# Ranking eight early steps by hand and loading the first units' queries without their zeros, in a kernel of chunked attention and a two-layer network

## The chip, the cores and the metric

The kernel runs on one core of one Trainium2 chip. A core has five engines, each with its own in-order queue: TensorE (PE, matmuls and their weight loads, the latter shown as PEld), VectorE (DVE), ScalarE (ACT), GpSimd (POOL) and SyncE (SP, which here only issues DMAs). They meet through semaphores. The metric is device time in microseconds (us), lower is better; the time before is the median of three runs.

## The reference

Attention over 4 batches, 8 heads, 768 positions, head size 64, in chunks of 32 queries; each chunk sees 8 memory keys, 16 positions to its left, itself and 8 to its right (at most 64 keys). The result, as 3072 tokens of 512 features, goes through a two-layer network of width 2048 with a leaky bend.

```python
for c in range(nc):
    l_start, r_end = max(0, c * 32 - 16), min(S, c * 32 + 40)
    k_full = concat([mem_k, k[:, :, l_start:r_end]]); v_full = concat([mem_v, v[:, :, l_start:r_end]])
    scores = matmul(q_c, k_full.T) / 8
    a = exp(scores - max(scores)); a = a / (sum(a) + 1e-09)
    out[:, :, c * 32:c * 32 + 32] = matmul(a, v_full)
x = out.transpose(0, 2, 1, 3).reshape(B * S, H * D)
h = x @ w_in
g = maximum(h, 0) + alpha * minimum(h, 0)
return g @ w_out
```

## The kernel before

**Units.** Attention is cut into 32 units: a pair of heads (4 pairs) by a block of 384 tokens (8 blocks, BT = 384). Four units fill x for one block. Units 0 to 7 (blocks 0 and 1) come first and go a way of their own, `windows` (L485 and on); the others are done in the shadow of the later matmuls.

**What a first unit goes through** (function `windows`): scores on PE (L307, 24 matmuls, ahead of them "stirs", L293, dummy matmuls on a tile of ones whose number is in STIR: eight for unit 0, two for others); `top`, a row maximum, on DVE (L504); `less`, the subtraction, on DVE (L508); `exps` on ACT (L512); `total` and `inverse` on DVE (L516, L519); `scale` on POOL in two steps (L529, L533); `turn`, one stir and six transposes on PE (L541); `keep`, two copies on ACT (L546); `values`, 16 matmuls on PE (L554); then x is split on ACT into a high part (L469) and on DVE into the low rest (L472). Units share buffers: score banks, exponentials, transposed weights and the tiles that `keep` fills are used in turn by even and odd units, and the loaded tile `early` by every fourth.

**A first unit's loads** (`load_first`, L485): one DMA of 1312 columns by 128 rows, the queries spread over two heads with zeros between them (768 columns, NQ) and the keys (544); another of 512 columns with the values. Keys and queries stand in DRAM as the kernel wants them, zeros included (array `first`, made in `_layout`). The score matmul takes 64 columns of the queries as its weights, contiguous in `early`: 32 queries of one head, 32 of the other, whose rows hold zeros where the other head's queries are.

**The weights** of the network come as 64-bit numbers, two DMAs for each of 16 slices f (w_in and w_out, L594), and are decoded on ACT and DVE: `rebias` (L617), `gather` (L625), `ends` (L629), `join` (L633), `high` (L641), `low` (L644). For f = 0 and 1 the two halves are decoded apart.

**The network.** Each place in ORDER is one (block, f): `up` (first layer, L718), `below` on ACT (L727), `bend` on DVE (L730), `high` and `low` (L736, L740), `down` (second layer, L748). Places 0 and 1 are f = 0 for blocks 0 and 1, places 2 and 3 are f = 1, and so on.

**Who sets the order.** Nothing runs in the order of the text. Every piece is a step of class `Plan`: engine, a cost, reads, writes, a due time. `Plan.send` gives each step a rank, the longest sum of costs and lags behind it, at least its due time; a user behind a DMA counts 2.3 us for the landing, one on another engine 0.07. Then it plays the plan: the engine that is free first takes, among its steps that are ready, the one of highest rank, the lower number where ranks are equal. What comes out is each engine's queue, which the chip runs in order. The steps are numbered in the order in which they are added: loads of units 0 to 3 and of the weights first, then unit by unit.

Of the kernel before, what the change touches and what calls it, by code (L numbers as in the profile page):

```python
# [18 lines left out]
P = 128  # L19
B, H, S, D = 4, 8, 768, 64  # L20
NM = 8
CH, LEFT, RIGHT = 32, 16, 8
# [3 lines left out]
NJ = TQ // CH  # L26
TK = LEFT + TQ + RIGHT
BT = 384
NHALF = B * S // BT
NT = BT // TQ  # L30
NPAIR = H // 2
# [36 lines left out]
NKT = TK + 2 * NM  # L68
STARTS = (0, LEFT + CH // 2, TK - 2 * CH + 2 * NM)

PE, DVE, ACT, POOL, SP = "PE", "DVE", "ACT", "POOL", "SP"
# [28 lines left out]
FIRST_FRONT = 12  # L100


STIR = (8, 2, 1)

DUE_WEIGHTS, LAST_OUT = 4, 8


NWIN, NSET = 2 * NPAIR, 4

STARTS_WIN = (0, 2 * LEFT, NKT - KW)  # L110
NQ = NT * NJ * 2 * CH
NV = NT * 2 * D
# [2 lines left out]


GATHER_ACT, HIGH_ACT = range(2, 14), 24


class Plan:  # L120
# [19 lines left out]
    def send(self):  # L140
        users = [[] for _ in self.steps]
        for n, step in enumerate(self.steps):
            for d in step[3]:
                users[d].append(n)
        lag = {PE: HOP, DVE: HOP, ACT: HOP, POOL: HOP, SP: LAND}
        behind = [0.0] * len(self.steps)
        for n in reversed(range(len(self.steps))):
            engine, cost, _, _, rest = self.steps[n]
            behind[n] = max(rest, cost + max((behind[m] + lag[engine] for m in users[n]), default=0.0))
        left = [len(step[3]) for step in self.steps]  # L150
        ready = [0.0] * len(self.steps)
        free = dict.fromkeys(lag, 0.0)
        able = {n for n in range(len(self.steps)) if not left[n]}
        while able:
            at = {}
            for n in able:
                engine = self.steps[n][0]
                at[engine] = min(at.get(engine, 1e9), max(ready[n], free[engine]))
            engine = min(at, key=at.get)
            n = max((n for n in able if self.steps[n][0] == engine and ready[n] <= at[engine]),  # L160
                    key=lambda n: (behind[n], -n))
            able.remove(n)
            _, cost, fn, _, _ = self.steps[n]
            free[engine] = at[engine] + cost
            fn()
            for m in users[n]:
                wait = lag[engine]
                if self.steps[m][0] == engine:
                    wait = FOLLOW if engine == DVE else 0.0
                ready[m] = max(ready[m], free[engine] + wait)  # L170
                left[m] -= 1
                if not left[m]:
                    able.add(m)
# [3 lines left out]
def body(ctx: ExitStack, tc: tile.TileContext, qvw, kw, first, w_in, w_out, alpha, out):  # L177
    nc = tc.nc
# [22 lines left out]
    qk = [const.tile([P, BT + NT * NKT], F32, name=f"qk{i}") for i in range(NKB)]  # L201
# [5 lines left out]
    early = [wps[NF - NSET + i, 0].tile([P, NQ + NT * NKT + NV], F32, name="early", tag="w") for i in range(NSET)]  # L207
# [7 lines left out]
        nc.gpsimd.memset(e[:, :, KW:], 1e-9)  # L215
    for ew in ews:
        nc.gpsimd.memset(ew, 0.0)
    warm = sm.tile([P, 1], F32, name="warm")
    nc.vector.memset(warm, 0.0)
    nc.scalar.activation(out=warm, in_=warm, func=AF.Exp)  # L220
# [2 lines left out]
    step = plan.add  # L223
# [20 lines left out]
    def rest(place):  # L244
        wide = NNARROW * NF
        return (len(ORDER) - max(place, wide)) * WIDE_PAIR + max(wide - place, 0) * PAIR

    def begins(u):

        return u // NPAIR if u < NWIN else BEGIN[(u - NWIN) // 2]  # L250

    def due(u, later=0):

        return rest(begins(u) + later + (5.5 if u >= FIRST_FRONT else 0))
# [35 lines left out]
    def stir(t, num):  # L290

        for _ in range(num):
            nc.tensor.matmul(out=t, lhsT=busy[:, :P], rhs=busy, start=True, stop=True)  # L293

    def score_products(u):
        blk, pr = divmod(u, NPAIR)
        st = state[u]
        s_ps = ps_s.tile([P, 512], F32, name="s_ps", tag=f"s{u % 2}")
        stir(s_ps, STIR[0] if u == 0 else STIR[1])
        st["s"] = s_ps[:, :2 * NJ * KW].rearrange("p (n k) -> p n k", k=KW)  # L300
        t = early[u % NSET]
        q = t[:, :NQ].rearrange("p (c x) -> p c x", c=NT * NJ)
        keys = t[:, NQ:NQ + NT * NKT].rearrange("p (t k) -> p t k", t=NT)
        for n in range(2 * NJ):
            for i in range(2):
                t, j = n // NJ * 2 + i, n % NJ
                nc.tensor.matmul(  # L307
                    out=st["s"][i * 2 * CH:(i + 1) * 2 * CH, n],
                    lhsT=q[:, t * NJ + j],
                    rhs=keys[:, t, STARTS_WIN[j]:STARTS_WIN[j] + KW],  # L310
                    start=True, stop=True,
                )
# [167 lines left out]
    def load_first(u):  # L480
        blk, pr = divmod(u, NPAIR)
        t = early[u % NSET]

        def load(lo, hi):
            nc.sync.dma_start(out=t[:, lo:hi], in_=first[blk, pr, :, lo:hi])  # L485

        state[u] = {}
        step(SP, 1.6, partial(load, 0, NQ + NT * NKT), writes=[("qk", u % NSET)], rest=due(u))
        step(SP, 0.78, partial(load, NQ + NT * NKT, NQ + NT * NKT + NV), writes=[("fv", u % NSET)], rest=due(u))

    def windows(u):

        st = state[u]
        sk, tks, ak = ("s", u % 2), [("o", 0), ("o", 1)], ("o", 2) if u % 2 else "a"
# [41 lines left out]
        def turn():  # L536
            st["t"] = [ps_o.tile([P, DM], F32, name="o_ps", tag=f"o{i}") for i in range(2)]
            stir(st["t"][0], STIR[2])
            for t in range(2):
# [8 lines left out]
        def values():  # L548
# [3 lines left out]
            for t in range(NT):  # L552
                for h2 in range(2):
# [4 lines left out]
                        start=True, stop=True,  # L558
                    )

        step(PE, 1.2, partial(score_products, u), reads=[("qk", u % NSET)], writes=[sk], rest=due(u))
        step(DVE, 0.66, top, writes=[sk, ("mx", u % 3)])
        step(DVE, 0.55, less, reads=[sk, ("mx", u % 3)], writes=e_keys(u))
        step(ACT, 0.52, exps, writes=e_keys(u))
# [24 lines left out]
    def load_w(f):  # L589
        def load(i):  # L590
            k, j = ((f, i), 0) if f < NAPART else ((f, 0), i)
            if k not in raw:
                raw[k] = wps[k].tile([P, 2 if f >= NAPART else 1, DM, 2], I32, name="w_t", tag="w")
            nc.sync.dma_start(out=raw[k][:, j].rearrange("p m b -> p (m b)"), in_=srcs[i][f])  # L594

        i = f - NF + NSET
        after = [("qk", i), ("fv", i)] if i >= 0 else []
        for i in range(2):
            step(SP, 1.31, partial(load, i), writes=[("r", f, i)] + after, rest=rest(place_of(f)))

    def place_of(f):
        return PLACE[0, f]
# [302 lines left out]
def _layout(q, k, v, mem_k, mem_v, moe_w_in, moe_w_out, moe_alpha):  # L905
    import numpy as np

    nh = S // BT
    qT = q.reshape(B, NPAIR, 2, nh, BT, D).transpose(0, 3, 1, 2, 5, 4)
    pad = ((0, 0), (0, 0), (LEFT, RIGHT), (0, 0))  # L910
    kp, vp = np.pad(k, pad), np.pad(v, pad)

    def keys(x, mem, s, *spans):
        return np.concatenate([mem if p is None else x[:, :, s + LEFT + p[0]:s + LEFT + p[1]] for p in spans], axis=2)

    kwin = np.stack([keys(kp, mem_k, t * TQ, (-16, 16), None, (16, 72), None, (72, 104)) for t in range(S // TQ)],
                    axis=2)
    kwin = kwin.reshape(B, NPAIR, 2, nh, NT, NKT, D).transpose(0, 3, 1, 2, 6, 4, 5)
    vwin = np.stack([keys(vp, mem_v, t * TQ, (-16, 16), None, (16, 104)) for t in range(S // TQ)], axis=2)
    vwin = vwin.reshape(B, NPAIR, 2, nh, NT, P, D).transpose(0, 3, 1, 5, 4, 2, 6)  # L920
    nwin = NWIN // NPAIR
    qd = np.zeros((nwin, NPAIR, 2, D, NT * NJ, 2, CH), q.dtype)
    for h in range(2):
        qd[:, :, h, :, :, h] = qT.reshape(NHALF, NPAIR, 2, D, NT * NJ, CH)[:nwin, :, h]
    kfirst = np.stack([keys(kp, mem_k, t * TQ, (-16, 16), None, (16, 104), None) for t in range(S // TQ)], axis=2)
    kfirst = kfirst.reshape(B, NPAIR, 2, nh, NT, NKT, D).transpose(0, 3, 1, 2, 6, 4, 5)
    kfirst = kfirst.reshape(NHALF, NPAIR, P, NT * NKT)[:nwin]
    vparts = vwin.reshape(NHALF, NPAIR, P, NV)
    return dict(
        qvw=np.concatenate([qT.reshape(NHALF, NPAIR, P, BT), vparts], axis=3),  # L930
        kw=np.ascontiguousarray(kwin).reshape(NHALF, NPAIR, P, NT, NKT),
        first=np.concatenate([qd.reshape(nwin, NPAIR, P, NQ), kfirst, vparts[:nwin]], axis=3),
        w_in=np.ascontiguousarray(moe_w_in.reshape(NK, P, NF, P).transpose(2, 1, 0, 3)
                                  ).reshape(NF, P, NK * P).view(np.int64),
        w_out=np.ascontiguousarray(moe_w_out.reshape(NF, P, DM)).view(np.int64),
        alpha=np.ascontiguousarray(moe_alpha.reshape(NF, P).T),
    )
# [15 lines left out]
```

## Time and profile before

| | us |
|---|---|
| median of 3 runs (599.72 to 600.05) | 600.02 |
| the profiled execution, whole | 600.83 |
| its span, first to last instruction | 599.0 |
| PE busy in the span | 592.1 |
| DVE, ACT, POOL busy | 388.2, 211.1, 36.7 |
| HBM read, MB | 41.95 |

The profile is of one execution, and its time of 600.83 us lies around a span of 599.0 us. A row of the order of time reads: start, length, engine, line of the kernel, operation, out<-in, shape, number of instructions, and in brackets the idle time of the engine just before and what ended it. A row of the DMA issues gives the kilobytes of each and the median time from issue to landing. A row by stretches gives for each engine the busy time within a window. The granted TensorE clock was 1.00 in the whole span.

### The profile page before, as it was taken

Reading aid. Unit: us, or ns where it says so; the run is one execution under the profiler, and the core shown is the slowest. Engines: PE = TensorE matmul, PEld = TensorE weight load, DVE = VectorE, ACT = ScalarE, POOL = GpSimd, SP = SyncE. Lnnn points to the kernel's source line nnn. Section 1 sums busy time; section 2 is a strip of 40 time slices with the busy share of each in tenths; the row PEclk is TensorE's granted clock in tenths of the full one; section 3 lists DMA queues with packets and bytes.
Section 4 is the critical chain, followed back from the end, with each engine's and each line's share of the span. In section 5 each row is a group of like instructions: output and inputs, shape, how many; then the busy total and the mean of one; then the engine's idle time right before and its main releaser. Section 6 shows DMA issues by size and latency. Waiting matters only on the chain.

```text
span 599.0 us, 10981 instructions
## 1 busy us (share of the span) xinstructions
PE 592.1 (99%) x4430; PEld 506.3 (85%) x4430; DVE 388.2 (65%) x904; ACT 211.1 (35%) x580; POOL 36.7 (6%) x61
## 2 busy tenths in 40 slices
PE   8999999999999999999999999999999999999997
PEld 5689898988988989899898888888888888888886
DVE  5888998887958768785885852861762771530530
ACT  3688878644222414323233301302400411210201
POOL 3410000010001101010010100100100100000000
PEclk9999999999999999999999999999999999999999
DMA  8999500222040302403204003003201000000001
GB/s 325 354 402 407 236 0 1 66 65 89 2 146 8 100 5 98 143 11 100 84 17 143 11 1 92 9 0 101 69 2 36 0 1 36 36 1 0 1 1 71
DMA packets 21076, 48.96 MB, mean 82 GB/s; under 512 B 2464, under 2 KB 5792, under 8 KB 21024
## 3 DMA queue, kind: packets, MB, share of 16 engines
q1 hardware_dynamic: 20880, 48.12, 22.7%
q8 instruction: 35, 0.57, 0.4%
q10 hardware_dynamic: 144, 0.13, 0.1%
q14 instruction: 17, 0.14, 0.1%
HBM read 41.95 MB, written 6.29 MB: 81 GB/s over the span
## 4 chain that ended last, share of the span: by engine, by line
PE 96%; DMA 2%; DVE 1%; ACT 1%; issue 0%; SPq 0%; ACTq 0%
PE h_ps L718 44%; PE o_ps L748 44%; PE a_ps L433 3%; PE s_ps L332 2%; DMA w_t<-w_in 2%; PE s_ps L293 1%; PE s_ps L307 1%; PE a_ps L554 0%; DVE w_t L629 0%; ACT qk L546 0%; PE o_ps L541 0%; ACT a L617 0%; DVE w_t L625 0%; DVE xl L472 0%; SPq L485 0%
## 5 line engine op out<-in xcount | busy, mean ns | idle before, releaser
L718 PE MATMUL h_ps<-xh,w 128*128 128x384 f32 (+1 forms) x896 | 248.8, 359 | 0.3 <-DVE w L644 0.3
L718 PEld LDWEIGHTS h_ps<-xh,w 128*128 128x128 f32 x896 | 164.8, 188 | 16.6 <-DVE w L644 0.6
L748 PE MATMUL o_ps<-w,gh 128*128 128x512 f32 x528 | 162.7, 389 | 0.0
L718 PE MATMUL h_ps<-xl,w 128*128 128x384 f32 (+1 forms) x448 | 162.6, 363 | 0.1
L727 ACT ACTIVATE g<-h_ps 128x384 f32<-128x384 f32 (+1 forms) x112 | 60.7, 542 | 194.4 <-PE h_ps L718 128.6
L730 DVE SCALAR_TENSOR_TENSOR g<-g,rise,h_ps 128x384 f32<-128x384 f32 (+1 forms) x112 | 74.8, 668 | 74.5 <-ACT g L727 73.6
L748 PEld LDWEIGHTS o_ps<-w,gh 128*128 128x128 f32 x528 | 99.1, 188 | 20.4
L408 DVE STREAM_TRANSPOSE pt<-e 32x64 f32<-32x64 f32 (+1 forms) x336 | 99.4, 301 | 7.4 <-POOL e L387 2.0
L748 PE MATMUL o_ps<-w,gl 128*128 128x512 f32 x264 | 102.8, 389 | 0.0
L718 PEld LDWEIGHTS h_ps<-xl,w 128*128 128x128 f32 x448 | 84.1, 188 | 10.2 <-DVE xl L472 0.3
L748 PE MATMUL o_ps<-w,xh 128*128 128x512 f32 x240 | 74.8, 393 | 0.0
L748 PEld LDWEIGHTS o_ps<-w,gl 128*128 128x128 f32 x264 | 49.6, 188 | 10.2
L472 DVE TENSOR_TENSOR xl<-a_ps,xh 128x384 fp32r<-128x384 f32 x32 | 17.7, 557 | 59.5 <-ACT xh L469 58.8
L748 PEld LDWEIGHTS o_ps<-w,xh 128*128 128x128 f32 x240 | 45.0, 188 | 8.9
L469 ACT CAST xh<-a_ps 128x384 fp32r<-128x384 f32 x32 | 15.0, 481 | 95.7 <-PE a_ps L433 93.7
L736 DVE CAST gh<-g 128x512 fp32r<-128x512 f32 (+1 forms) x72 | 28.8, 401 | 30.6 <-PE o_ps L748 28.2
L387 POOL TENSOR_TENSOR e<-e,den 128x384 f32<-128x384 f32 x24 | 22.7, 947 | 419.8 <-DVE den L384 270.0
L740 DVE TENSOR_TENSOR gl<-g,gh 128x512 fp32r<-128x512 f32 (+1 forms) x72 | 46.6, 648 | 1.7
L366 ACT ACTIVATE e<-s_ps,mx 128x64 f32<-128x64 f32 x144 | 43.4, 318 | 11.1 <-DVE mx L358 11.1
L748 PE MATMUL o_ps<-w,xl 128*128 128x512 f32 x120 | 46.8, 390 | 0.0
L366 ACT ACTIVATION_READ_ACCUMULATOR e<-s_ps,mx 128x1 f32 x144 | 30.4, 211 | 0.0
L805 ACT COPY o_t<-o_ps 128x512 f32<-128x512 f32 x21 | 12.2, 591 | 44.6 <-PE o_ps L748 44.1
(58 smaller groups left out, 382.6 us busy)
## 6 DMA issues: line engine op xcount, KB each, us to landing
w_t<-w_in SPq DMA_DIRECT2D x16, 512.0 KB, 10.1
w_t<-w_out SPq DMA_DIRECT2D x16, 512.0 KB, 10.0
qk<-kw SPq DMA_DIRECT2D x24, 272.0 KB, 4.4
v_t<-qvw SPq DMA_DIRECT2D x24, 256.0 KB, 2.9
out<-o_t SPq DMA_DIRECT2D x23, 256.0 KB, 2.1
early<-first SPq DMA_DIRECT2D x8, 656.0 KB, 6.3
qk<-qvw SPq DMA_DIRECT2D x24, 192.0 KB, 4.9
early<-first SPq DMA_DIRECT2D x8, 256.0 KB, 6.9
```

What stands on the lines that cost most here:

```text
L366: nc.scalar.activation(out=st["e"][:, i], in_=st["s"][h2][:, n], func=AF.Exp, scale=SCALE, bias=d["mx"][:, u - us[0], n, h2:h2 + 1], accum ...
L387: nc.gpsimd.tensor_tensor(out=st["e"], in0=st["e"], in1=st["den"].broadcast_to([P, NJ * 2, KW]), op=ALU.mult)
L408: nc.vector.transpose(out=pts[u % NPT][quad * CH:(quad + 1) * CH, j, t0:t0 + n1 - n0].rearrange("p t h q -> p (t h) q"), in_=(st["e"], zer ...
L433: nc.tensor.matmul(out=st["a"][h2 * D:(h2 + 1) * D, t * TQ:(t + 1) * TQ], lhsT=st["v"][:, t, h2, :], rhs=pts[u % NPT][:, :, t, h2, :], sta ...
L469: nc.scalar.copy(out=ring[k][0][:, cols], in_=st["a"][:, :BT])
L472: nc.vector.tensor_tensor(out=ring[k][1][:, cols], in0=st["a"][:, :BT], in1=ring[k][0][:, cols].bitcast(F32), op=ALU.subtract)
L718: nc.tensor.matmul(out=h["ps"][:, :n_cols], lhsT=ws[f, 0][:, wk, k * P:(k + 1) * P], rhs=parts(blk, k)[1](xk), start=(k == 0 and n == 0), ...
L727: nc.scalar.activation(out=h["g"], in_=h["ps"][:, :n_cols], func=AF.Relu, scale=-1.0)
L730: nc.vector.scalar_tensor_tensor(out=h["g"], in0=h["g"], scalar=rise[:, f:f + 1], in1=h["ps"][:, :n_cols], op0=ALU.mult, op1=ALU.add)
L736: copy(out=h["gh"], in_=h["g"])
L740: nc.vector.tensor_tensor(out=h["gl"], in0=h["g"], in1=h["gh"].bitcast(F32), op=ALU.subtract)
L748: nc.tensor.matmul(out=o_ps[tt], lhsT=h[gk][:, tt * P:(tt + 1) * P], rhs=ws[f, 1][:, wk], start=(f == first_f and i == 0), stop=(f == last ...
```

## The change

The queries of units 0 to 7 are stored in DRAM without zeros and loaded in two halves, one head's 64 rows each, into a tile whose other quarters are set to zero once by eight memsets on DVE. Inside the tile the queries of one column group now stand 12 columns apart, where they stood side by side. `load_first` adds four steps in place of two, with planned costs of 0.43 (three times) and 0.65 in place of 1.6 and 0.78; the score step waits for all three of its loads, and so does the weight load that later takes over the tile's place. The stirs ahead of unit 0's scores are seven. And after the ranks are worked out, eight steps get a number added to their own rank, by their step number: SHIFT.

```diff
-STIR = (8, 2, 1)
+STIR = (7, 2, 1)
...
+SHIFT = {11: -2.4, 14: -0.5, 53: -1.4, 92: -8.1, 137: -4.4, 188: 6.2, 195: 7.0, 231: -13.4}
...
             behind[n] = max(rest, cost + max((behind[m] + lag[engine] for m in users[n]), default=0.0))
+        for n, more in SHIFT.items():
+            behind[n] += more
...
+    for t in early:
+        for h2 in range(2):
+            nc.vector.memset(t[(1 - h2) * D:(2 - h2) * D, h2 * BT:(h2 + 1) * BT], 0.0)
...
-        q = t[:, :NQ].rearrange("p (c x) -> p c x", c=NT * NJ)
+        q = t[:, :NQ].rearrange("p (x c) -> p c x", c=NT * NJ)
...
-        def load(lo, hi):
-            nc.sync.dma_start(out=t[:, lo:hi], in_=first[blk, pr, :, lo:hi])
+        def load(rows, to, lo, hi):
+            nc.sync.dma_start(out=t[rows, to:to + hi - lo], in_=first[blk, pr, rows, lo:hi])
...
-        step(SP, 1.6, partial(load, 0, NQ + NT * NKT), writes=[("qk", u % NSET)], rest=due(u))
-        step(SP, 0.78, partial(load, NQ + NT * NKT, NQ + NT * NKT + NV), writes=[("fv", u % NSET)], rest=due(u))
+
+        for h2 in range(2):
+            step(SP, 0.43, partial(load, slice(h2 * D, (h2 + 1) * D), h2 * BT, 0, BT), writes=[("fq", h2, u % NSET)], rest=due(u))
+        step(SP, 0.43, partial(load, slice(0, P), NQ, BT, BT + NT * NKT), writes=[("qk", u % NSET)], rest=due(u))
+        step(SP, 0.65, partial(load, slice(0, P), NQ + NT * NKT, BT + NT * NKT, BT + NT * NKT + NV), writes=[("fv", u % NSET)], rest=due(u))
...
-        step(PE, 1.2, partial(score_products, u), reads=[("qk", u % NSET)], writes=[sk], rest=due(u))
+        step(PE, 1.2, partial(score_products, u), reads=[("qk", u % NSET)] + [("fq", h2, u % NSET) for h2 in range(2)], writes=[sk], rest=due(u))
...
-        after = [("qk", i), ("fv", i)] if i >= 0 else []
+        after = [("qk", i), ("fv", i), ("fq", 0, i), ("fq", 1, i)] if i >= 0 else []
...
+    qfirst = qT.reshape(NHALF, NPAIR, P, NT * NJ, CH)[:nwin].swapaxes(3, 4).reshape(nwin, NPAIR, P, BT)
...
-        first=np.concatenate([qd.reshape(nwin, NPAIR, P, NQ), kfirst, vparts[:nwin]], axis=3),
+        first=np.concatenate([qfirst, kfirst, vparts[:nwin]], axis=3),
```

By the order in which steps are added, the eight numbers are: 11, the second half of unit 2's queries; 14, the first half of unit 3's; 53, unit 0's `values`; 92, the first half of unit 6's queries; 137, the first `keep` of unit 5; 188, the `join` of w_in for f = 0; 195, the `high` of w_out for f = 0; 231, the `below` of place 2 (block 0, f = 1).

More of the change, by code (lines that the diff above doesn't have):

```diff
@@ L921, in _layout @@
     nwin = NWIN // NPAIR
-    qd = np.zeros((nwin, NPAIR, 2, D, NT * NJ, 2, CH), q.dtype)
-    for h in range(2):
-        qd[:, :, h, :, :, h] = qT.reshape(NHALF, NPAIR, 2, D, NT * NJ, CH)[:nwin, :, h]
+    qfirst = qT.reshape(NHALF, NPAIR, P, NT * NJ, CH)[:nwin].swapaxes(3, 4).reshape(nwin, NPAIR, P, BT)
     kfirst = np.stack([keys(kp, mem_k, t * TQ, (-16, 16), None, (16, 104), None) for t in range(S // TQ)], axis=2)
```

## The prediction

> **What bounds the kernel now.** I read the page first, then the busy time by stretches, then the chain of waits, and last the order of time of the first 40 us, engine by engine. The page says what carries the whole:
>
> ```profile
> PE 592.1 (99%) x4430; PEld 506.3 (85%) x4430; DVE 388.2 (65%) x904; ACT 211.1 (35%) x580; POOL 36.7 (6%) x61
> ...
> DMA  8999500222040302403204003003201000000001
> GB/s 325 354 402 407 236 0 1 66 65 89 2 146 8 100 5 98 143 11 100 84 17 143 11 1 92 9 0 101 69 2 36 0 1 36 36 1 0 1 1 71
> ```
>
> TensorE (PE) is 99% busy; the DMA engines are full only in the first four slices of 15 us. The stretches show where TensorE is not dense:
>
> ```profile
> 25.00:30.00 5.00, 4.69 (x52) 3.78 (x52) 4.78 (x12) 4.58 (x11) 2.60 (x5) 1.00 1.00 371
> 30.00:35.00 5.00, 4.88 (x52) 3.91 (x51) 4.93 (x9) 4.48 (x9) 2.33 (x5) 1.00 0.99 382
> ...
> 5.00:35.00 30.00, 28.28 (x391) 21.05 (x391) 24.40 (x58) 17.96 (x38) 11.88 (x27) 1.00 0.98 367
> 35.00:100.00 65.00, 65.00 (x340) 58.85 (x340) 57.44 (x81) 54.07 (x71) 0.00 (x0) 1.00 0.53 212
> 100.00:595.00 495.00, 495.00 (x3695) 425.29 (x3693) 305.88 (x765) 136.98 (x470) 22.72 (x24) 1.00 0.14 46
> ```
>
> Behind each length stand the busy times of TensorE, its weight loads, VectorE (DVE), ScalarE (ACT) and GpSimd, then the granted clock, the DMA share and GB/s. In the third row 30.00 - 28.28 = 1.72 us of TensorE are idle between 5 and 35 us, and none behind that. So the end is set by when TensorE gets into its dense run, and the change touches nothing later than that, but for one step. The chain of waits agrees:
>
> ```profile
> 10.15 9.20 DMA w_t<-w_in
> ...
> 36.32 2.28 PE h_ps L718 x12
> ...
> 573.49 21.77 PE o_ps L748 x96
> ```
>
> It runs through the landing of the first weights (9.20 us), then the units, and from 36.32 us through matmuls alone. What the change can give is therefore idle TensorE time before 36 us, plus TensorE work removed. These are the waits:
>
> ```profile
> 1.45 3.60 PE L293 MATMUL s_ps<-busy 128*128 128x512 bf16 x8 [1.45 <-DVE warm L219]
> 4.98 1.41 PE L307 MATMUL s_ps<-early 128*64 128x64 f32 x24
> ...
> 9.51 0.61 PE L293 MATMUL s_ps<-busy 128*128 128x512 bf16 x2 [0.27 <-DVE e L508]
> ...
> 12.29 0.60 PE L293 MATMUL s_ps<-busy 128*128 128x512 bf16 x2 [0.36 <-DVE e L508]
> ...
> 13.91 0.82 PE L541 MATMUL o_ps<-eye,ew 128*128 128x128 f32 x6
> 14.65 0.88 PE L554 MATMUL a_ps<-qk,early 128*64 128x96 f32 x16
> ...
> 18.11 0.88 PE L554 MATMUL a_ps<-qk,early 128*64 128x96 f32 x16 [0.21 <-DMA early<-first]
> ...
> 21.85 0.88 PE L554 MATMUL a_ps<-qk,early 128*64 128x96 f32 x16 [0.33 <-DVE den L516]
> ...
> 27.36 0.62 PE L718 MATMUL h_ps<-xh,w 128*128 128x384 f32 x2 [0.31 <-DVE w L644]
> ```
>
> Two waits for a free score bank (0.27, 0.36), two in the middle (0.21, 0.33), one for the decoded weights (0.31): 1.48 of the 1.72 us. The middle ones come from ACT, which works in order:
>
> ```profile
> 15.96 0.53 ACT L512 ACTIVATE e<-e 128x384 f32<-128x384 f32 x1
> 19.37 0.69 ACT L617 ACTIVATE a<-w_t 128x512 f32<-128x512 f32 x1 [2.89 <-DMA w_t<-w_in]
> 19.97 0.85 ACT L546 COPY qk<-o_ps 128x384 f32<-128x384 f32 x2
> ...
> 20.10 0.75 DVE L625 COPY w_t<-w_t 128x512 int16<-128x512 int16 x1 [1.66 <-ACT a L617]
> ```
>
> ACT stood 2.89 us before the first weights, with the copies of unit 2's turned weights (L546, 19.97) queued behind, and DVE then idled 1.66 us.
>
> **Part 1, the shorter loads.** What they have to do is in these rows:
>
> ```profile
> early<-first SPq DMA_DIRECT2D x1, 656.0 KB, 4.0
> ...
> early<-first SPq DMA_DIRECT2D x8, 656.0 KB, 6.3
> ...
> early<-first SPq DMA_DIRECT2D x8, 256.0 KB, 6.9
> ...
> 0.74 9.36 SPq L485 DMA_DIRECT2D early<-first  x9
> ...
> 10.15 0.42 SPq L594 DMA_DIRECT2D w_t<-w_in  x1
> ...
> w_t<-w_in SPq DMA_DIRECT2D x1, 512.0 KB, 9.2
> ```
>
> The 656 KB (1312 columns) become 96 + 96 + 272 KB (384 columns for 64 rows twice, 544 for 128). A unit loses 192 KB, eight lose 1536 KB. Ahead of the first w_in there were seven such loads and two of 256 KB (5104 KB); with the new ranks there are six units' 464 KB, 368 KB of unit 6 and two of 256 KB (3664 KB). 1440 KB at the 367 GB/s of 5 to 35 us is 4.0 us: w_in lands not at 10.15 + 9.2 = 19.35 but at about 15.3. The bound from below is SyncE (SP): 22 issues stand ahead of it instead of nine; at 0.42 us and a gap of some 0.05 that is about 10.4 us, hardly other than 10.15, and with the 4.0 us of the emptiest queue it is 14.4. The bound from above is 19.35. I take 15.3.
>
> The first unit landed at 0.74 + 4.0 = 4.74. Now its last load is issued two issues later (about 1.6) but ends a queue of 464 KB. Bounds: 0.9 us later (two issues, no gain in transfer) to 0.5 us earlier (192 KB at 367 GB/s). I take 0.4 earlier, since the same bytes less the zeros pass the same engines, and the issue lies beside the transfer.
>
> **Part 2, one stir fewer.** Eight stirs take 3.60 us, spaced by about 0.43 (4.98 - 1.45 = 3.53, over eight). Seven let the first scores start at 4.55, if the load is there; the estimate above says 4.34. Gain 0.43; none, if the load is as late as before.
>
> **Part 3, the zeros written on chip.** Eight memsets of 64x384 on DVE:
>
> ```profile
> L342 DVE MEMSET s_ps<- 32x32 f32 x12 | 1.0, 85 | 0.5
> ...
> L200 DVE MEMSET busy<- 128x512 bf16 x1 | 0.5, 485 | 0.9 <-PEq L944 0.9
> ...
> 6.47 0.07 DVE L500 MEMSET s_ps<- 64x16 f32 x1 [5.07 <-PE s_ps L307]
> ...
> 7.76 0.53 ACT L512 ACTIVATE e<-e 128x384 f32<-128x384 f32 x1 [5.54 <-DVE e L508]
> ```
>
> From 85 ns at 32 columns and 485 at 512, 0.83 ns a column: 0.38 us each, 3.0 in all, from 1.4 to 4.4 us. DVE idles 5.07 us there, so they cost nothing; the warm-up exp behind them moves to 4.4, and ACT idles until 7.76. Without that cover 3.0 us would be paid. The loads write other rows than the memsets of their columns, so none waits for another.
>
> **Part 4, the strided queries.** The weights of the score matmuls are now read with a step of 12 columns (48 B) in place of 1. No row shows such a read; the nearest is the present one:
>
> ```profile
> 6.85 0.78 PEld L307 LDWEIGHTS s_ps<-early 128*64 128x64 f32 x24 [0.42 <-DMA early<-first]
> 6.85 0.92 PE L307 MATMUL s_ps<-early 128*64 128x64 f32 x24
> ```
>
> Bounds: nothing, or twice the 0.78 us of weight load per unit, 8 x 0.78 = 6.2 us. A gain is excluded: the same columns are loaded. I take nothing in the likeliest case, because each of these 24 loads is paired with a matmul of the same 64 columns, and keep 6.2 us as a rival.
>
> **Part 5, the eight ranks.** load_first now adds four steps, so from each unit on the numbers shift by two more; counted out, they are these.
> - 11 and 14 (SP): one query half of unit 2 and one of unit 3 go behind unit 3's other two loads: at most two issues, 0.9 us later. They are issued by 6.4 (twelve issues), and unit 2's scores come behind two units' scores and a pair of stirs, not before 7.5 (4.55 + 1.41 + 0.61 + 0.92). Nothing; 0.9 if that were shorter.
> - 92 (SP): a query half of unit 6 falls by 8.1, from beside its keys to behind alpha. SP's first w_in is 0.42 us earlier. The half stands seven issues behind it, at about 14; unit 6's scores come behind unit 0's values (53), past 17. Nothing.
> - 53 (PE): unit 0's value matmuls (0.88 us) fall behind unit 5's stirs and scores and unit 2's transposes. Behind them wait x of unit 0, SP's load of unit 4's values and, since both use one buffer, ACT's copies for unit 2, hence unit 3's transposes. From the old start, 14.65, about 0.9 sooner, come stirs and scores (0.61 + 0.92), transposes with their stir (1.0) and the values (0.88): 17.2. Then the copies take 0.85 and their hand-over some 0.15 more, beside unit 1's value matmuls (0.88): I put 0.15 us against it.
> - 137 (ACT): the first copy for unit 5 falls behind unit 3's and 4's x; unit 6's transposes wait for it. Cover: TensorE has first-layer matmuls ready by then. Nothing; its price is one ACT step, 0.5 us, if they are not.
> - 188 and 195 (DVE, ACT): the join of w_in and the high part of w_out, both of f = 0, go ahead of unit steps. The wait of 0.31 us at 27.36 for the low part, which ran at 26.46, goes.
> - 231 (ACT): the below of place 2 falls by 13.4, behind decoding. TensorE has no idle in 35 to 100, so it is covered; else one step of 0.5 us.
>
> ```profile
> 26.46 0.85 DVE L644 TENSOR_TENSOR w<-a,w 128x512 fp32r<-128x512 f32 x1
> ...
> 10.30 0.55 POOL L533 TENSOR_TENSOR ew<-e,den 128x112 f32<-128x112 f32 x2
> ...
> 11.15 0.56 DVE L504 TENSOR_REDUCE mx<-s_ps 128x6 f32<-128x384 f32 x1
> ...
> 11.72 0.52 DVE L508 TENSOR_TENSOR e<-s_ps,mx 128x384 f32<-128x384 f32 x1
> ```
>
> One order changes unasked. With unit 3's loads later in the plan, DVE takes unit 2's less (11.72) ahead of unit 3's top (11.15). It may start when GpSimd is done with unit 0 (10.85), so the bank for unit 4's scores is free some 0.8 us sooner. Of 0.27 + 0.36 us I count 0.45. By the same planner the rebias of w_in stands ahead of unit 4's exp on ACT, no longer behind it; ACT comes there at about 15.1 (15.96 less the 0.43 and 0.45), against a landing at 15.3. So the stall of 2.89 us and its two waits (0.21 + 0.33) go.
>
> **The sum.** 0.43 + 0.45 + 0.54 + 0.31 - 0.15 = 1.58, say 1.6 us. The profiled execution took 600.83 us (span 599.0): it would be 599.2. It lies 0.81 above the median of the runs, 600.02, so the forecast there is **598.4**. At most the 1.72 us, the stir and some 0.5 us that lie under the modelled ends of matmuls go (transposes and values stand 0.74 apart undisturbed, from 13.91 to 14.65, and further at the two waits): 2.7 us, 597.3. What is late next is DVE, busy 4.78 and 4.93 of 5 us from 25 to 35; its work starts earlier by the 1.66 us that it stood at 20.10, so it permits the 1.6.
>
> **The rivals.**
> - The halves transfer at half speed, and the stall only moves. For it: ahead of w_in the bytes fall by 1440 KB, of which 13 x 96 are such halves; if each took twice its time, 1248 KB or 3.4 of the 4.0 us would come back, and w_in would land at 18.7. ACT would then wait from 15.1 with unit 4's exp behind it, which was done by 16.49 and now would end near 20. Against it: two halves on different rows can overlap. The stall of 3.6 us is 0.7 longer than the 2.89; with 0.43 and 0.31 kept I get no change, 600.0. Beyond a landing of about 17.5 nothing of the gain is left. The Trainium skill has this rule in "SBUF — State Buffer", section "Door 1: the DMA port swizzle": 64 rows reach half of the ports, and two such loads do not add up. Every load in the trace has 128 rows, so no row here bears on it.
> - The gain is made and given back: ACT is busy 4.58 of 5 us from 25 to 30 and DVE nearly all of it; if the later copy for unit 5 or the place-2 step holds TensorE, 1.0 of the 1.6 is lost: 599.4. Against it: no TensorE wait there before but the 0.31.
> - Slower: the strided weight loads take longer. At double, 6.2 us of TensorE work, less all idle and the stir (1.72 + 0.43 + 0.5): 3.6 us, 603.6. It decides from some 0.33 us per unit (2.65 / 8), a load 42% longer. For it: scores are bound by these loads and TensorE is nearly full; against it: the load runs beside a matmul. The Trainium skill says in "Advanced Engine Details and Errata", section "Memory Cachelines", that accesses which hit a different 16-byte line each time pay a penalty; by that rule a step of 48 B would pay on every column. No run here shows it yet.
>
> **How the numbers follow.** Likeliest case 0.60 (598.4, between 597.3 and 599.2), half speed 0.17 (600.0), given back 0.11 (599.4), strided 0.12 (603.6). 0.2%, about what a measurement of this kernel can tell, is 1.2 us: below 598.8 is faster, above 601.2 slower. Faster: nine tenths of the likeliest and a little of the third, 0.57. Same: the rest of the likeliest, most of the half speed and the third, 0.29. Slower: the strided case and the bad end of half speed, 0.14. The range runs from 597.3 to 601.0, which leaves out the strided case and little else.
>
> **What would show it.** Right: first scores at about 4.55 with score weight loads still 0.78 us for 24; unit 2's less before unit 3's top; w_in landed by 16 and ACT's wait there below 0.5 us; the low part of w_in done by 24; TensorE's first dense run begins 1.6 us sooner than 36.32. Wrong: PEld of L307 over 1.0 us, w_in after 17.5, or a new TensorE wait over 0.5 us between 14 and 40 us, most likely before unit 3's or unit 6's transposes.

## The result and the profile after

The changed kernel takes 606.75 us (median of four runs, 605.90 to 607.73) beside 600.03 us for the kernel before, run on the same chip: a ratio of 1.0108 (95% interval 1.0095 to 1.0121). It is slower by 6.7 us, where 1.6 us less were forecast. The profiled execution after took 607.73 us, with a span of 605.9. Of the four runs two, this one among them, show a mean granted clock of 0.994 and 0.996 and took 607.73 and 607.09 us, while the two at 1.000 took 606.42 and 605.90, 1.25 us less on the mean, so that this profile overstates the loss a little.

From the page of the kernel after, the busy times of the whole span; then, from the busy times by line, the row of the score matmuls after, and under it the same row of the kernel before:

```profile
PE 597.9 (99%) x4426; PEld 513.7 (85%) x4429; DVE 389.0 (64%) x912; ACT 210.7 (35%) x580; POOL 36.8 (6%) x61
```

```profile
L316 PE MATMUL s_ps<-early 128*64 128x64 f32 x192 | 14.9, 313 | 2.6 <-DMA early<-first 1.5 <-DVE warm L228 0.9
```

```profile
L307 PE MATMUL s_ps<-early 128*64 128x64 f32 x192 | 7.8, 235 | 0.0
```

TensorE's busy time grew from 592.1 to 597.9 us and its idle time in the span from 6.9 (599.0 - 592.1) to 8.0 (605.9 - 597.9): of 6.9 us more span, 5.8 are work and 1.1 are waiting. Nearly all of the work is in one line, the 192 score matmuls: 7.8 us before, 14.9 after (L307 has become L316). The transposes add 0.7 (6.5 to 7.2), in the stretch with the lower clock. The 7.1 us of the row are more than the 5.8 of the sum, because the rows of the stirs and of the value matmuls are shorter and because the modelled end of such a row lies over the start of the next.

The busy times by stretches after, with the columns that the prediction explained:

```profile
5.00:10.00 5.00, 4.48 (x51) 3.67 (x52) 1.78 (x7) 0.73 (x2) 0.00 (x0) 1.00 0.91 245
10.00:15.00 5.00, 3.53 (x38) 2.57 (x38) 2.97 (x9) 0.53 (x1) 1.12 (x3) 0.62 1.07 272
15.00:20.00 5.00, 4.67 (x50) 4.11 (x49) 1.79 (x7) 1.91 (x4) 2.25 (x6) 0.70 1.05 331
...
5.00:35.00 30.00, 27.53 (x313) 23.02 (x317) 16.89 (x47) 12.69 (x27) 7.47 (x19) 0.89 0.89 270
```

The DMA engines are as full as before (0.91, 1.07, 1.05) and move less: 245 and 272 GB/s from 5 to 15 us. DVE and ACT, which stood at 24.40 and 17.96 us of work between 5 and 35 us, do 16.89 and 12.69 there, because what they wait for comes later. The granted clock, the column ahead of the DMA share, is 0.62 and 0.70 from 10 to 20 us. The order of time of TensorE after, the score matmuls of the first four units and the first transposes:

```profile
1.45 3.12 PE L302 MATMUL s_ps<-busy 128*128 128x512 bf16 x7 [1.45 <-DVE busy L206]
5.52 1.85 PE L316 MATMUL s_ps<-early 128*64 128x64 f32 x24 [0.94 <-DVE warm L228]
...
7.84 1.84 PE L316 MATMUL s_ps<-early 128*64 128x64 f32 x24
...
11.47 1.90 PE L316 MATMUL s_ps<-early 128*64 128x64 f32 x24 [1.47 <-DMA early<-first]
...
16.50 1.49 PE L553 MATMUL o_ps<-eye,ew 128*128 128x128 f32 x6 [0.33 <-POOL ew L545]
```

24 score matmuls take 1.85 us where they took 0.92; unit 0 starts at 5.52 in place of 4.98, and unit 2 waits 1.47 us for a load. The new chain of waits begins in SyncE's queue:

```profile
0.73 0.57 SPq L494
1.35 0.58 SPq L494
...
6.03 0.58 SPq L494
6.65 4.78 DMA early<-first
11.47 1.91 PE s_ps L316 x24
...
43.34 2.80 PE h_ps L730 x15
```

The last row is the first stretch of the network with no unit in it: it begins at 43.34, where that of before began at 36.32. The 7.0 us are the whole loss of this profile; behind it TensorE is dense in both. Ahead of it stand ten issues, 0.59 us apart on the mean (0.73 to 6.65) where 0.47 was reckoned (0.42 and a gap), then half a unit's queries of 96 KB, 4.78 us on the way, then scores. How the weights stand behind them is in SyncE's rows:

```profile
0.73 13.77 SPq L494 DMA_DIRECT2D early<-first  x22
14.55 0.43 SPq L606 DMA_DIRECT2D w_t<-w_in  x1
...
20.97 0.33 SPq L606 DMA_DIRECT2D w_t<-w_out  x1
```

The first w_in is issued at 14.55 (10.15 before). The issue at 20.97 is the one that the trace lets wait for w_in's landing, 1.5 us: it landed just ahead of that, 1.6 us later than the 19.35 of before. Two orders of the forecast did come:

```profile
14.49 0.55 DVE L520 TENSOR_TENSOR e<-s_ps,mx 128x384 f32<-128x384 f32 x1
...
16.35 0.56 DVE L516 TENSOR_REDUCE mx<-s_ps 128x6 f32<-128x384 f32 x1
```

Unit 2's `less` (14.49) runs ahead of unit 3's `top` (16.35), and TensorE no longer waits for a score bank; but only because the scores themselves are what is late.

### The profile page after: what moved, and what is told of

It is laid out like the page before. It is cut to its first block, busy times and chain, and to the rows that moved or that the text cites. A ratio compares the mean times of both kernels' runs of the same rounds, so it can differ in the third digit from the quotient of the medians.

```text
span 605.9 us, 11007 instructions
## 1 busy us (share of the span) xinstructions
PE 597.9 (99%) x4426; PEld 513.7 (85%) x4429; DVE 389.0 (64%) x912; ACT 210.7 (35%) x580; POOL 36.8 (6%) x61
## 4 chain that ended last, share of the span: by engine, by line
PE 97%; SPq 1%; DMA 1%; issue 0%; POOL 0%; DVE 0%; ACT 0%; POOLq 0%; ACTq 0%
PE h_ps L730 44%; PE o_ps L760 43%; PE a_ps L442 3%; PE s_ps L341 2%; PE s_ps L316 1%; PE o_ps L553 1%; PE a_ps L566 1%; SPq L494 1%; DMA early<-first 1%; PE o_ps L302 0%; PE s_ps L302 0%; POOL ew L541 0%; ACT o_t L817 0%; DVE e L520 0%; POOL ew L545 0%
## 5 line engine op out<-in xcount | busy, mean ns | idle before, releaser
L481 DVE TENSOR_TENSOR xl<-a_ps,xh 128x384 fp32r<-128x384 f32 x32 | 17.5, 552 | 59.4 <-ACT xh L478 58.7
```

The costliest lines, as they stand in the source:

```text
L481: nc.vector.tensor_tensor(out=ring[k][1][:, cols], in0=st["a"][:, :BT], in1=ring[k][0][:, cols].bitcast(F32), op=ALU.subtract)
```

## The experiments

Three theories were to be told apart: **the step** (the weights of the score matmuls, read 48 B apart, load at half the rate), **the halves** (loads of 64 rows run slowly and are issued slowly) and **the ranks** (the numbers in SHIFT move a step into the way). In every comparison below the kernel before was run on the same chip as the kernel beside it.

**1. The step alone.** The kernel before, full loads and zeros, with the query columns laid out 12 apart:

```diff
-        q = t[:, :NQ].rearrange("p (c x) -> p c x", c=NT * NJ)
+        q = t[:, :NQ].rearrange("p (a x s) -> p a s x", s=12, x=2 * CH)
...
-                    lhsT=q[:, t * NJ + j],
+                    lhsT=q[:, (t * NJ + j) // 12, (t * NJ + j) % 12],
...
```

> The kernel before, with nothing changed but where its queries stand in the tile: full loads with zeros, eight stirs, no ranks, and score weights read with a step of 12 columns (48 B). Theory stride (reading the weights with that step doubles the score matmuls and is the bulk of the loss): 24 score matmuls take about 1.84 us as in the changed kernel, not 0.92; eight units are 7.0 us of TensorE, less idle of up to 1.7: 605.2 to 607.0. Theory half loads (loads of 64 rows run at half speed, scores wait for them, the clock falls): 600 to 601. Theory ranks: 600.

Measured: 605.72 us against 600.19, ratio 1.0090 (1.0073 to 1.0107). The step by itself costs 5.5 us. The rows of line L307 (shortest, median and longest of one in ns), matmuls and weight loads:

```profile
L307 PE MATMUL s_ps<-early x192: 293/300/396, 5.0 to 29.5; 128*64 128x64 f32 x192
L307 PEld LDWEIGHTS s_ps<-early x192: 207/237/243, 5.0 to 29.4; 128*64 128x64 f32 x192
```

A weight load of 64 columns takes 237 ns; before it took 138:

```profile
L307 PEld LDWEIGHTS s_ps<-early x192: 132/138/232, 5.0 to 23.8; 128*64 128x64 f32 x192
```

**2. From which step on.** The same with a step of 2 columns (8 B) and of 4 (16 B), s=2 and s=4 in the diff above.

> The kernel before with its full loads, eight stirs and no ranks; only the weights of the score matmuls are read with a step of 2 columns (8 B) in place of 1. Known: a step of 12 columns (48 B) took 1.84 us for the 24 matmuls of a unit in place of 0.92 and made 605.7 of 600.2. Line theory (each 16-byte line that is fetched costs, and two columns share one at 8 B): about half of the loss per unit, 0.4 to 0.5 us, 8 x 0.45 = 3.6 less some 1.7 us of hidden waits, 602 to 603. Any-step theory (every read that is not contiguous goes at half rate): 1.84 us per unit and 605 to 606. Distance theory (the cost grows with the step in bytes): under 1.05 us per unit and 600 to 601.

> The same with a step of 4 columns (16 B): no two neighbouring columns share a 16-byte line any more. Line theory: the full loss, 1.84 us per unit as at 48 B, 605 to 606. Any-step theory: the same 605 to 606. Distance theory: a third of the loss, about 1.2 us per unit, 601 to 602.5.

At 8 B: 600.26 us against 600.34, ratio 1.0000 (0.9991 to 1.0009). At 16 B: 604.51, ratio 1.0070 (1.0055 to 1.0085). The weight loads at 8 B, then at 16 B:

```profile
L307 PEld LDWEIGHTS s_ps<-early x192: 136/138/140, 4.9 to 23.3; 128*64 128x64 f32 x192
```

```profile
L307 PEld LDWEIGHTS s_ps<-early x192: 192/217/219, 5.0 to 28.2; 128*64 128x64 f32 x192
```

138, 138, 217 and 237 ns at steps of 4, 8, 16 and 48 B. Loads overlap (24 of 138 ns would be 3.3 us and keep the line busy for 0.78), but the busy time of a unit says the same: weight loads 0.78, 0.80, 1.52 and 1.71 us, scores 0.92, 0.94, 1.66 and 1.84. Not every read that isn't contiguous pays (any-step falls), the cost doesn't grow evenly with the distance (distance falls), and it isn't half paid at 8 B, as I had put it for the lines: it is nothing that the time shows at 8 B and four fifths of the whole at 16 B ((217 - 138) / (237 - 138)). The Trainium skill has this rule in "Advanced Engine Details and Errata", section "Memory Cachelines": lines of 16 bytes, and two hits on a line are needed to hide the latency of the memory. The trace agrees as to where the cost sets in: two columns to 16 bytes at 8 B (600.26 us, nothing lost), one at 16 B (4.2 us lost). Why 48 B costs another 20 ns a load the rule doesn't say; steps of 12 and 32 B were not tried, and other data types neither.

**3. The change without its step.** The kernel after, halves, memsets, ranks and seven stirs kept, with the weights read contiguously. These are other columns than the right ones, so the attention of the first units is another computation, of the same size.

```diff
-        q = t[:, :NQ].rearrange("p (x c) -> p c x", c=NT * NJ)
+        q = t[:, :NQ].rearrange("p (c x) -> p c x", c=NT * NJ)
```

> The changed kernel with the score weights read side by side as before, everything else kept: half loads, memsets, ranks, seven stirs. It changes the computation: the scores of the first eight units are formed from the wrong columns. Theory stride: scores take 0.92 us again and the time falls by most of the loss, to 599 to 601. Theory half loads: the waits for loads (1.47 us before unit 2's scores) and the clock at 0.6 to 0.7 stay, 603 to 606. Theory ranks: 605 to 607.

Measured: 602.94 us against 600.19, ratio 1.0049 (1.0034 to 1.0064), between what the theory of the step (599 to 601) and that of the halves (603 to 606) gave. The granted clock stayed at 1.00. The rest of the change costs 2.75 us where it was to bring 1.6. Its waits, in the order of time of TensorE:

```profile
5.24 0.92 PE L316 MATMUL s_ps<-early 128*64 128x64 f32 x24 [0.63 <-DMA early<-first]
...
7.68 0.92 PE L316 MATMUL s_ps<-early 128*64 128x64 f32 x24 [0.98 <-DMA early<-first]
...
11.01 0.57 PE L316 MATMUL s_ps<-early 128*64 128x64 f32 x12 [1.17 <-DMA early<-first]
...
21.82 0.38 PE L302 MATMUL o_ps<-busy 128*128 128x512 bf16 x1 [1.57 <-ACT qk L558]
...
24.08 0.92 PE L316 MATMUL s_ps<-early 128*64 128x64 f32 x24 [0.80 <-DMA early<-first]
```

The four longest waits for loads, those of units 0, 1, 2 and 6, and the stall on ACT: 5.15 us. (Read contiguously, the first 12 matmuls of a unit need only the first half of its queries, so unit 2 starts before its wait.) The stall has its source in w_in, for which ACT waits longer than the 2.89 us of before:

```profile
20.33 0.66 ACT L629 ACTIVATE a<-w_t 128x512 f32<-128x512 f32 x1 [3.56 <-DMA w_t<-w_in]
```

With the step as well, TensorE waits only 0.94 + 1.47 + 0.33: it is busy with slow scores while the loads land. That is why 5.5 and 2.75 do not add up to 8.25 but to 6.7.

**4. Without the ranks, and the ranks alone.** The kernel after with SHIFT empty; and the kernel before with the five numbers of SHIFT that are no query halves, at the steps that they name there.

```diff
-SHIFT = {11: -2.4, 14: -0.5, 53: -1.4, 92: -8.1, 137: -4.4, 188: 6.2, 195: 7.0, 231: -13.4}
+SHIFT = {}
```

```diff
+SHIFT = {45: -1.4, 121: -4.4, 172: 6.2, 179: 7.0, 215: -13.4}
...
+        for n, more in SHIFT.items():
+            behind[n] += more
```

> The changed kernel with none of the eight ranks moved. Theory stride and theory half loads: within 1 us of the changed kernel, 605.8 to 607.8. Theory ranks (the moved steps, above all unit 0's values behind unit 5's scores and unit 2's and 3's loads pushed back, are the bulk): 600 to 603.

> The kernel before with the five moved ranks that are not loads (unit 0's values, the first keep of unit 5, the join and the high of f = 0, the below of place 2); the three of query halves have no step here. Theory ranks: 602 or more. Theory stride and theory half loads: 599 to 600.5; by the terms of the prediction the join and the high are worth up to 0.3 us, the moved values cost 0.15.

Without the ranks: 607.70 us, ratio 1.0125 (1.0109 to 1.0140); the interval overlaps that of the change, so the eight ranks can't be told from nothing there, and the theory that they are the bulk falls. Five of them alone: 601.08, ratio 1.0014 (1.0005 to 1.0024), 0.9 us slower, between the two expectations. TensorE's order has one row that the profile before has not:

```profile
43.66 0.50 PE L753 MATMUL o_ps<-w,xl 128*128 128x512 f32 x1 [0.46 <-DVE xl L745]
```

The second layer waits there for the low part of g (L745), which DVE had behind decoding; the forecast took the network steps of this stretch as covered, because TensorE had no idle time there. How much of the 0.9 us this wait makes is not shown. Waits of the same kind, 0.41 and 0.33 us, stand in the profile without ranks at 58.00 and 60.65; and with the five ranks unit 1's scores already start 0.40 us later than before (7.25, not 6.85), ahead of every moved step. Which of the five costs the time was not tried apart. The profile without ranks has another thing: unit 2's scores follow unit 1's without a wait, at 10.13. So the ranks made the 1.47 us of the kernel after, most likely rank 11, which puts half of unit 2's queries behind unit 3's loads; it was not moved alone.

**5. The zeros left out without halves, and with them.** To part the halves from the step, the scores are computed by 48 matmuls of one head (64 rows, 32 contiguous columns) in place of 24. Then the queries need no zeros and lie compact behind one another, and may be loaded with the keys in one DMA of 464 KB by 128 rows, or in halves. All else is as in the kernel before.

```diff
-NQ = NT * NJ * 2 * CH
+NQ = BT
...
-                nc.tensor.matmul(
-                    out=st["s"][i * 2 * CH:(i + 1) * 2 * CH, n],
-                    lhsT=q[:, t * NJ + j],
+                for h2 in range(2):
+                    rows = slice(h2 * D, (h2 + 1) * D)
+                    nc.tensor.matmul(
+                        out=st["s"][(2 * i + h2) * CH:(2 * i + h2 + 1) * CH, n],
+                        lhsT=q[rows, t * NJ + j],
...
```

> The kernel before, with the zeros left out in another way: the queries stand compact in DRAM and are loaded with the keys in one DMA of 928 columns by 128 rows (464 KB in place of 656), and the scores are 48 matmuls of one head each (64 rows, 32 columns of weights, contiguous) in place of 24. No half loads, no memsets, eight stirs, no ranks. Theory of the shorter load (fewer bytes on 128 rows do free the queue): w_in lands by 17, ACT's wait of 2.89 us before it goes below 1.5 us, and if the 48 narrower matmuls take the 0.92 us of the 24, 599.0 to 599.8. Rival (narrow matmuls cost as much each): 1.4 to 1.9 us per unit, 8 x 0.5 to 1.0 = 4 to 8 less hidden waits, 603 to 606.

> As the kernel with 48 matmuls of one head, with the same bytes loaded in three DMAs, as the change does it: two halves of the queries by 64 rows (96 KB each) and the keys (272 KB), with the planned costs 0.43 each. No memsets, no step, no ranks, eight stirs. Half-load theory (64 rows at half the rate, and longer issues on SyncE): w_in lands 2 to 4 us later than with the one load, waits for DMAs of 1.0 us or more stand before the scores of units 1 to 3, and it is 1.5 to 3 us slower than the one load. Rival (what was slow in the change's loads came from the memsets and the planner's order): within 0.6 us of the one load.

> As the kernel with 48 matmuls of one head and halves, but the two halves of the queries are one DMA of 128 rows (192 KB, 1536 B a row), and the keys stay apart (272 KB, 2176 B a row): the same bytes, the same piece per row, two issues in place of three, no DMA of 64 rows. Known: with halves 605.1 and w_in landed at 20.80; with everything in one DMA of 128 rows 599.9 and w_in at 16.63. Theory of the 64 rows (a DMA of 64 rows keeps only a part of the engines' width busy and takes longer to issue): near the one load, w_in by 17.5, no wait for early over 0.4 us before the first four scores, 600 to 601. Rival (small pieces per row are slow, whatever the rows): near the halves, w_in after 19.5 and 603 to 605.

One load: 599.87 us against 600.34, ratio 0.9990 (0.9981 to 1.0000); the 48 narrow matmuls take 0.88 us a unit, no more than the 24, so they cost nothing and the rival falls. Two halves and the keys: 605.12 (603.95 to 606.43), ratio 1.0087 (1.0070 to 1.0103). Queries in one DMA of 128 rows and the keys: 600.56 against 600.38, ratio 1.0005 (0.9995 to 1.0014). The stretches from 5 to 15 us, first with the halves, then with two DMAs of 128 rows:

```profile
5.00:10.00 5.00, 3.67 (x105) 2.33 (x108) 2.72 (x8) 0.53 (x1) 0.00 (x0) 1.00 0.86 234
10.00:15.00 5.00, 3.71 (x107) 2.34 (x107) 2.38 (x9) 1.55 (x4) 1.97 (x5) 1.00 1.00 268
```

```profile
5.00:10.00 5.00, 4.18 (x156) 2.95 (x162) 3.44 (x11) 1.05 (x2) 0.42 (x1) 1.00 1.03 372
10.00:15.00 5.00, 3.90 (x111) 3.05 (x110) 3.43 (x11) 1.37 (x3) 2.88 (x9) 1.00 1.05 382
```

The same bytes in the same pieces per row (1536 B of queries, 2176 B of keys) move at 234 and 268 GB/s in halves and at 372 and 382 in whole rows, with the DMA engines 0.86 and 1.00 busy in halves, 1.03 and 1.05 in whole rows. So it is the 64 rows and not the size of the pieces, and the rival of the last expectation falls. SyncE's first rows, halves and then whole rows:

```profile
0.73 4.75 SPq L487 DMA_DIRECT2D early<-first  x8
```

```profile
0.74 4.65 SPq L487 DMA_DIRECT2D early<-first  x10
```

0.59 us an issue against 0.47. Three issues of 0.59 us for the 464 KB of a unit hand out some 267 GB/s at most (an estimate from this row), about the rate of the stretches above; how much of the loss is slow issue and how much slow transfer these runs don't part. And the landing of w_in, by ACT's wait for it, with one load, two and halves:

```profile
16.65 0.68 ACT L619 ACTIVATE a<-w_t 128x512 f32<-128x512 f32 x1 [0.54 <-DMA w_t<-w_in]
```

```profile
15.70 0.68 ACT L620 ACTIVATE a<-w_t 128x512 f32<-128x512 f32 x1 [2.71 <-DMA w_t<-w_in]
```

```profile
20.82 0.66 ACT L621 ACTIVATE a<-w_t 128x512 f32<-128x512 f32 x1 [2.62 <-DMA w_t<-w_in]
```

16.65 with one load, 15.7 with two, 20.8 with halves, where it was 19.35 with the zeros. (The kernel with one load and seven stirs, below, has the same loads and 17.96, so that two profiles with like loads differ by 1.3 us.) With two DMAs w_in is issued a unit's loads earlier, at 8.49 and not 10.44, and lands ahead of the one load; its profile has waits of 0.73 us for unit 4's load and of 1.26 us that no row explains, and its time is that of before. Halves undo more than the missing zeros bring. The halves' kernel was expected 1.5 to 3 us behind the one load; it is 5.25 behind. The Trainium skill's "DMA: Bandwidth & Descriptors", section "Rules for kernel authors", advises against two transfers to the two halves of the partitions, since they share the same engines one after the other, and for one of 128; the rates of 234 and 372 GB/s agree.

**6. The stir, and the best version.** Seven stirs in the kernel before, and seven in the kernel with one load and 48 matmuls.

```diff
-STIR = (8, 2, 1)
+STIR = (7, 2, 1)
```

> The kernel before with seven stirs ahead of unit 0 in place of eight and nothing else. The forecast put 0.43 us on it if the load is there, and the first load of before lands at 4.72 to 4.74. Theory: scores of unit 0 start at 4.8 in place of 4.98, 0.2 us or less, 599.9 to 600.3, no change to be measured. Rival (the stir is worth its whole time): 599.7.

> The kernel with 48 matmuls of one head and one load of 464 KB, with seven stirs ahead of unit 0 in place of eight: the removal of the zeros without halves, step, memsets or ranks. Theory of the forecast's first terms (a load that lands early lets the shorter stir count whole): first scores at 4.55 in place of 4.98, 0.43 us off 599.9, 599.4; 598.4 if the wait of 1.06 us in the middle of unit 1's values, which no row explains, does not come again. Rival (the first scores wait for something else by then, or the wait moves): 599.7 to 600.1, no change to be measured.

Before with seven stirs: 600.19 us against 600.38, ratio 1.0001 (0.9992 to 1.0010). One load with seven stirs: 599.87, ratio 0.9992 (0.9983 to 1.0001). Both are no change that can be measured. The first scores and the wait that came up, with full loads:

```profile
4.67 1.21 PE L307 MATMUL s_ps<-early 128*64 128x64 f32 x24
...
8.19 0.92 PE L307 MATMUL s_ps<-early 128*64 128x64 f32 x24 [0.53 <-DMA early<-first]
```

And with one compact load:

```profile
4.55 1.51 PE L309 MATMUL s_ps<-early 64*32 64x64 f32 x48
5.99 0.13 PEld L293 LDWEIGHTS <-busy 128*128 128x128 bf16 x2 [0.17 <-issue]
...
6.39 0.47 PE L293 MATMUL s_ps<-busy 128*128 128x512 bf16 x1 [0.33 <-issue]
```

With full loads the scores do start sooner, at 4.67, and stand again at 8.19, 0.53 us for unit 2's load (somewhat less if, as it seems, the record of a stir is missing ahead of it): the stir was cover for that load, and its 0.43 us only moved. With the compact load they start at 4.55, as forecast. The 0.33 us at 6.39 are most likely no wait: the program has two stirs there, the weight loads of both are recorded (x2 at 5.99) and the matmul of one only, so that a record seems to be missing.

In the profile of the version with one load and eight stirs stands a wait that has no such gap in the records, in the middle of unit 1's values:

```profile
19.03 0.55 PE L556 MATMUL a_ps<-qk,early 128*64 128x96 f32 x8 [1.06 <-issue]
```

It isn't in the profile with seven stirs, though the two times are alike, 599.87 both; there TensorE waits 0.49 us for DVE at 34.06 instead. So what it costs is not shown, and whether it and the 1.26 us with two DMAs come from the 192 more pairs of instructions was not tried and stays open. No version beat the kernel before by more than the intervals allow.

## Why the prediction was wrong

**Part 4 is the step that failed.** It took nothing for the strided weight loads in the likeliest case, with the reason that each is paired with a matmul of the same 64 columns. The pairing hides nothing here: the row that the prediction itself quoted, 0.78 us of weight load in 0.92 us of scores, shows loads that fill the line almost alone, and a longer load must show. After, from the same view:

```profile
7.83 1.71 PEld L316 LDWEIGHTS s_ps<-early 128*64 128x64 f32 x24 [0.42 <-DVE s_ps L512]
```

0.93 us more of loads (1.71 - 0.78), and 0.92 more of scores (1.84 - 0.92): all of it shows. By itself that made 5.5 us (experiment 1). The rival had the mechanism, the place, the sign and, with at most 6.2 us of work, nearly the price; 7.1 us of matmul time came. It went wrong in the cover: it let idle time and the stir take 2.65 us off, for 3.6 in all, and in experiment 1 some 6.9 us more of scores (7.8 to 14.7 by line) cost 5.5. It had the point from which it decides, 0.33 us per unit, and its chance of 0.12 was far too small beside a row that showed scores as bound by these loads. Nothing in the trace of before bore against it.

**Part 1 failed as well.** The 1440 KB fewer ahead of w_in were divided by 367 GB/s, the rate of loads of 128 rows; the halves ran at 245 and 272. w_in landed at about 20.9, not 15.3, and issues came 0.59 us apart or more, where 0.47 was taken. So the stall that was to go grew: without the step ACT waits 3.56 us for w_in (experiment 3). The first unit, put 0.4 us earlier at 4.34, came later: its scores wait for the load until 5.24 there. The half-speed rival had the kind and stopped at 18.7 and at no change; it left out that slower issues and transfers also delay the units that run before w_in is needed, which is where the waits of 0.63, 0.98 and 1.17 us in experiment 3 stand. Even the zeros left out cleanly would not have given the 4.0 us: w_in landed at 16.65 and 17.96 with one load.

**Part 2** held as a time of one stir (first scores at 4.55 with a compact load) and failed as a gain: with full loads it moved to unit 2's load (experiment 6). In the change itself the first scores came at 5.52.

**Part 3** was right in the cost and nearly in the cover: eight memsets of 378 ns, but 0.49 us apart, so that they end at 5.43 and not at 4.4. They release unit 0's scores by the trace; with halves and no memsets these start at 5.37 all the same, so the memsets cost 0.15 us at most.

**Part 5.** The order of `less` and `top` came as worked out. Ranks 11 and 14 were put at nothing by setting the time at which their halves are issued (by 6.4) against the time at which unit 2's scores can start (7.5). That leaves out the way: with the 4.0 us that the prediction itself gives to the emptiest queue, the half lands at 10.4. In the kernel after it is issued at 6.65, is 4.78 us on the way, and unit 2 waits 1.47, which it does not do without the ranks. The five ranks that are not loads were not free either: by themselves they cost 0.9 us. As a whole the ranks can't be told from nothing within the change.

**The sum.** The two middle waits and the bank waits did go, and so did ACT's stall (its rebias of w_in waits for nothing after), all because TensorE became the last to arrive: with fast scores the stall is there (experiment 3). The forecast also named what is late next, DVE; with one load and no step, where its Parts 1 and 2 were nearest to true, the time fell by 0.5 us at most, hardly to be told from nothing, of 1.6; its profiles still have waits for DVE and one that no row explains. What would show it wrong was named rightly: a PEld of L307 over 1.0 us (1.71 came), w_in after 17.5, and new waits over 0.5 us.

## What to carry to other kernels

Where matmuls are small, look at the weight loads' share of their line first: if it is near the whole, the layout of the stationary operand is a price and not a detail, and a step has to be priced: here, in fp32, one of 8 B was free and one of 16 B was not. Saving bytes by splitting a load over the two halves of the rows can cost more than the bytes were worth; the same saving in transfers of 128 rows did not. A load counts when it has landed, not when it is issued. And a rule that speaks against a change, with no row of the trace on the other side, should weigh as the likeliest case and not as a rival.

## What the runs showed of the hardware

- Weight loads of 64 columns in fp32: 138 ns at a step of 4 and 8 B, 217 at 16 B, 237 at 48 B.
- Loads of 64 rows, alternating with keys of 128: 234 to 268 GB/s with DMA engines 86% to 100% busy, against 372 to 382 in whole rows; 0.59 us an issue against 0.47.
- 48 matmuls of 64 rows by 32 columns took 0.88 us, no more than 24 of 128 by 64 (0.92).
- The granted clock fell to 0.62 and 0.70 from 10 to 20 us in the profile after, where the wait of 1.47 us lies, and six transposes took 1.49 us in place of 0.82. What lowered it stays open: the profile without ranks, which has no such wait, shows 1.00 throughout these stretches, but so does that of experiment 3, with waits of up to 1.57 us.
